# Weight sums on GpSimd instead of VectorE, with all units and loads in a new order: an attention and gated feed-forward kernel

## The chip, the cores and the metric

The kernel runs on one core of a Trainium2 chip. The metric is the device time of one execution in microseconds (us); three runs were made of the kernel before. A profile is one further execution, recorded instruction by instruction. PE is TensorE (matmuls), PEld its weight loads, DVE VectorE, ACT ScalarE, POOL GpSimd, SP SyncE, which here only issues DMAs.

## The reference

Eight batches with 12 heads of 448 tokens and 64 dimensions go through an attention without softmax, and the result through a gated feed-forward layer with exact GELU:

```
scores = (q @ k.T) / sqrt(64)
attn   = max(scores, 0) ** 2 / 448
x      = attn @ v                      # 12 heads x 64 = 768 columns, 3584 rows
out    = (gelu(x @ w_gate) * (x @ w_val)) @ w_out   # 768 -> 1536 -> 768
```

Inputs and output are float32; the kernel computes in bf16 with float32 accumulation.

## The kernel before, in words

**Attention.** For each batch `b`, heads are worked in pairs and in three groups `m` of four heads. q and k come by a casting DMA issued from GpSimd into `qk16`. They are transposed into `qkT`: for the first six groups by TensorE (line 683, against the identity `ident`) with a copy on VectorE or ScalarE (line 687), for the later ones by a regrouping copy on VectorE (line 511, `qkr`) and two DMA transposes issued by SP (line 516). A scores unit (`s` in the order, 21 per batch) makes 128 x 896 scores in PSUM; ScalarE applies relu (line 751), in batch 0 VectorE for the units in `RELU_V` (line 749); VectorE squares in place (line 770), two units in one instruction, in batch 0 only for the numbers in `PAIRED`. A values unit (`v`, one per head pair) multiplies by v; VectorE or ScalarE scales the result into `xT` (lines 829 and 841).

**Feed-forward.** All weights stay in SBUF: `w_gate` and `w_val` in six pieces `wg0..5`, `wv0..5` of 256 columns, loaded in pairs (`W` in the list of loads), and `w_out` in four pieces `wo0..3` (`O`). A digit in the order is a plain gate or value unit of that batch: gate ends in a GELU on ScalarE (line 1104), value in a product on VectorE into `uT` (line 1109). For batches 2 to 7 part of this work is done by a seven-product scheme on 2 x 2 blocks (units such as `2A1`): instead of eight block products seven are made, of sums of blocks. That needs sums of weights, `ws`: four per weight pair, made in `add_pair_sums` (line 905, 24 instructions of 128 x 768 in all), and sums of tokens, `ts` (line 934). The fourth sum of each pair is written over the upper half of `wv` itself, so it waits until the plain units that read that half are done.

**Output.** The product with `w_out` uses the same scheme in 14 groups `a` to `n` of 256 rows, seven units each; it needs sums of output weights, `wt` (line 1152, eight instructions of 128 x 1152, in two chains of four), and sums of `uT`, `s` (line 1236). ScalarE copies and VectorE adds into `osb` (lines 1319 and 1317), and SP stores it.

**TensorE.** Every matmul uses a 64 x 64 quarter of the array, four side by side; nearly all are recorded on line 401, in `mm`. Two streams, `PE0` and `PE1`, are interleaved: the lower half of one unit beside the upper half of another. Where nothing is ready in the first 24 us, `fill` issues matmuls on the zero tile `warm` (line 603) so that TensorE does not sit idle.

**What sets the order.** It is planned while the program is built. `START` and `LINE` list the units; `LOADS` lists the first DMAs, which GpSimd issues in order. `run_plan` simulates the engines with a cost per operation and emits each instruction on its engine when the plan says it starts; on the chip each engine then runs its instructions in that order, and semaphores hold it where an input is late. From 12 units ahead it takes the first that is ready. Loads of late batches are paced: each waits on GpSimd for a relu of an earlier batch (`op.behind`). A DMA transpose is taken to land 5 us after its issue (`lag=5.0`).

Of the kernel before, what the change touches and what calls it, by code (L numbers as in the profile page):

```python
# [12 lines left out]
s s s 0 0 s t s 0 s s v 0 s s s s t s v 0 0 0 v 0 s s s s s v s v 0 s s 0 s v 0 1 0 0 1 1 1 1 s 1 0  # L13
0 1 0 s s 1 0 s s s 1 s 1 1 w1 v s s 1 1 s 0 1 1 1 0 s 1 s s 0 1 0 s s 0 1 v 1 1 1 1 a1 s a2 s s s
a7 a6 1 v a4 s a5 v s b7 s b1 s b6 v w0 a3 s s b5 b4 b2 s v 2 s b3 s 2 s 2 s 2 v 2 s 2 s s s s v s
s s v 2 s 2 2 c1 c6 v c7 s s v 2 c2 c4 2 c5 s s 2 v s s 2A1 2D1 s 2A7 2D7 w2 2A2 2A6 c3 s s s 3 2D6
2A5 2A4 v 2D2 2D4 s 3 v 2D5 2F1 s 2E1 2F2 2A3 3 s 2F6 s 2D3 2E7 2F7 s 2E6 v 2E2 2E5 2E4 2E3 3 s 2C1
2F5 s 3 2C6 2F4 2B1 2C2 v 2C7 2B6 2B7 2C5 s s s 2F3 2B5 s 2C4 s 3 2C3 w3 s s s 2B2 s 2B4 3 2B3 3 d1
d7 d6 3 3 v v s s e1 s s e2 d5 e7 d4 d3 v d2 s s s e6 v s f7 3 s 3 s f1 e4 f6 s s f5 e5 s s 4 f4 4
v s s f3 v f2 4 4 v s s e3 s s 4 4 4 s s s g7 v 4A1 s g1 s s s s v v g6 4 5 s 4A7 4A2 4A6 g5 g2 g4  # L20
4D1 4A4 s s 4E1 4A5 4E2 v s 4A3 4D7 g3 4D6 4E6 s 4D5 4D2 5 4E7 4E4 s 4B1 4E5 s s 4F1 s 4B6 v 4D4
4D3 s s 4B7 v 4B2 4G1 4B5 4B4 s 4F6 4F7 4F2 4G6 4E3 4B3 4G2 s 4H1 s 4F5 4F4 4F3 4G7 v 4C1 s s 4H2
4H7 4G5 4H6 4G4 s 4H4 4H5 s 4G3 s 4C6 s v v 4C7 4C5 4C2 5 4C4 s s 4C3 s 5 5 h7 4H3 h1 s 5 5 s h6 s
h5 i1 5 i7 s i6 s v s s s h3 v i4 h2 6B1 h4 v 6A1 s s v 6B2 i5 i3 6A6 6A2 j1 j7 j2 i2 6A7 6B7 6D1
6G1 6A4 6B6 j6 j4 6A5 6B4 w4 6D7 j5 6D6 6B5 6G6 6G7 6A3 6D2 w5 6G5 j3 6G2 6C1 6C2 6B3 6C6 6D4 6E1
6D5 6E2 6C7 6H1 6G4 6C5 6C4 6E7 6D3 6G3 6E6 6H2 6L1 6H7 6E5 6H6 6H4 6K1 6H5 6C3 6L2 6K2 6L6 6E4 6K6
6L7 6L5 6H3 6K7 6F1 6I1 6E3 6F6 6F7 6J1 6F2 6K5 6K4 6F5 6L4 6I2 6I6 6F4 6J6 6I7 6L3 6J2 6J7 6K3 6F3
6I5 6I4 6J5 k7 6J4 6I3 6J3 l1 n1 l6 k1 k6 k5 k4 k3 l7 l4 m7 m1 m2 n7 n2 m6 l5 l3 n6 m4 m5 n5 n4 l2
m3 n3 k2
# [3 lines left out]
LOADS = "q8 v4 v8 W0 Q0 W1 Q1 V0 W2 V1 Q2 W3 V2 W4 W5 O0 O1 O2 O3"  # L33
# [3 lines left out]
t00a s0 s1 t01 s2 s3 s4 s5 s6 t10 s7 t11 s8 s9 s10 t20 t21 s11 v0 s12 s13 v1 s14 v2a s15 s16 x0 v3a  # L37
s17 x0 s18 x1 x1 x1 s19 v4a s20 f x0 x0 x0 x1 v5 t30
# [3 lines left out]
class Op:  # L42
# [4 lines left out]
    def __init__(self, engine, cost, emit, deps=(), lag=0.0, prio=0, other=None):  # L47
        self.serial = Op.count
        Op.count += 1
        self.engine, self.cost, self.emit, self.prio = engine, cost, emit, prio  # L50
        self.deps = [d for d in deps if d is not None]
        self.lag = lag
        self.other = other
        self.takes = None
        self.margin = 0.0
        self.after = None
        self.gate = 0.0
        self.hold = self.whole = False
        self.mark = None
        self.start = self.end = self.known = self.blocked = None  # L60
# [58 lines left out]
def run_plan(queues, pools, units, banks, full, arrivals, together, fill, blocks, span):  # L119

    free = {e: 0.0 for e in (*queues, *pools)}
    at = {e: 0 for e in queues}
# [4 lines left out]
    def ready(op):  # L129
        if op.known is not None:  # L130
            return op.known
        if op.blocked is not None and op.blocked.end is None:
            return None
        t = 0.0
        if op.after is not None:
            if op.after.start is None:
                return None
            t = op.after.start
        if op.takes is not None:
            x = op.takes[0].free(*op.takes[2:])  # L140
            if x is None:
                return None
            t = max(t, x)
        for d in op.deps:
            if d.end is None:
                op.blocked = d
                return None
            t = max(t, d.end + d.lag + (op.margin if d.engine == "SP" else 0.0))
        if op.gate:
            if not blocks.marks:  # L150
                return None
            at, _ = blocks.marks[-1]
            t = max(t, at, free[op.engine])
# [12 lines left out]
        return t  # L166
# [51 lines left out]
    while left:  # L218
# [16 lines left out]
        for e, ops in pools.items():  # L235
            mine = None
            for op in ops[:48]:
                r = ready(op)
                if r is not None:
                    t = max(r, free[e], floor if e in together else 0.0)  # L240
                    key = (t, op.prio, free[e])
# [38 lines left out]
        free[e] = op.end  # L280
# [27 lines left out]
def kernel(  # L308
# [38 lines left out]
    PAIRED = (0, 7)  # L347
    RELU_V = (0, 16)
    GATE_T, BLOCK = 0, 7.1

    NPB = (0,0,3,3,4,4,6,6)
    TWO = 2, 4, 6
# [5 lines left out]
    RING_M, RING_G = 5, 4  # L358

# [20 lines left out]
           for i in range(FB)]  # L380
    early = tc.tile_pool(name="psS1", bufs=1, space=bass.MemoryType.PSUM)
    psS.append(early.__enter__())

    ctx.enter_context(tc.manual_schedule())

    ident = const.tile([128, 128], bf16)
    warm = const.tile([128, 512], bf16, name="warm")
# [22 lines left out]
    ACT, DVE, POOL, SP, IDLE = [], [], [], [], []  # L410
# [91 lines left out]
    def add_dma_transposes(b, m, deps=()):  # L502
# [34 lines left out]
        if m and b == EARLY:  # L537
            tr_op[b, m][0].deps.append(tr_op[b, m - 1][1])
# [9 lines left out]
    held, readers, until, shut = {}, {}, {k: 0.01 * k - 1e3 for k in range(FB)}, {}  # L548
# [13 lines left out]
    def new_bank(k, reader, shape=(128, 512), dtype=f32):  # L562
        if k >= FB and len(psF) == FB:
# [6 lines left out]
    def next_scores(at):  # L570

        n = len(units)
        if n >= WIDE and n % SB == 0 or wide:
# [5 lines left out]
        return n % SB, units[n - SB:n - SB + 1]  # L579

    def scores_read(n, reader):
        units.append(reader)
        if n == 1:
            for k in (FB, FB + 1):
                readers[k] = [reader]

    def fill(t0, t1):
# [3 lines left out]
        at_rest = {k: -1.0 if held.get(k) is None else held[k].end for k in (*range(FB), *held)}  # L591
# [288 lines left out]
    def add_pair_sums(i):  # L880
# [18 lines left out]
        for n, x, y, op in ((1, lambda: a21, lambda: a22, ALU.add),  # L899
# [5 lines left out]
            have = [Op("DVE", 0.53, lambda n=n, x=x, y=y, op=op: nc.vector.tensor_tensor(  # L905
                made(n), x(), y(), op=op), have, lag=0.2, prio=3)]
            ws_op[n, i] = have[0]
            DVE.extend(have)
# [15 lines left out]
    def add_token_sums(b):  # L924
# [3 lines left out]
        def emit(n, x, y, op):  # L928
# [5 lines left out]
            nc.vector.tensor_tensor(ts[b, n][:, :, :], x, y, op=op)  # L934

        b11, b12, b21, b22 = (b0, KTOP, c0), (b1, KTOP, c1), (b0, KEND, c0), (b1, KEND, c1)
        for n, x, y, op, on in ((3, b22, b12, ALU.subtract, []), (1, b12, b11, ALU.subtract, [3]),
# [4 lines left out]
            made = Op("DVE", 0.83 if b in TWO else 0.48, lambda n=n, x=x, y=y, op=op: emit(n, x, y, op),  # L942
# [8 lines left out]
            DVE.append(made)  # L951
# [3 lines left out]
    def add_pair(at, b, unit, name):  # L955
# [8 lines left out]
        if name in opens:  # L964
            st["box", stage] = {}
            free = []
        else:
            free = [st["read", stage]]
# [13 lines left out]
        def emit(r, k):  # L982
# [62 lines left out]
        if name in "167":  # L1045
# [19 lines left out]
        then(at, GS, *ops, box if name in opens else None, lambda: st["read", stages_last[stage]])  # L1065
# [73 lines left out]
    def add_weight_sums():  # L1139

        for i in range(2):
# [6 lines left out]
            for n, out_, x, y, op in ((3, wt[3, i][:, :, :], b22, b12, ALU.subtract),  # L1148
# [3 lines left out]
                done = Op("DVE", 0.75, lambda out_=out_, x=x, y=y, op=op: nc.vector.tensor_tensor(  # L1152
# [3 lines left out]
                DVE.append(done)  # L1156
# [39 lines left out]
    def add_sums(gr):  # L1196
# [26 lines left out]
        def add(n, x, y, op, into=None, after=(), cuts=(0, KH)):  # L1223
# [3 lines left out]
            def emit(f0, f1):  # L1227
# [4 lines left out]
                for j in ((0, 1) if split else (None,)):  # L1232
# [3 lines left out]
                    nc.vector.tensor_tensor(st["tile"][n][:, f0:f1, cols], a, c, op=op)  # L1236

            for f0, f1 in zip(cuts, cuts[1:]):
# [161 lines left out]
    for n, (b, m) in enumerate(late):  # L1400
# [3 lines left out]
        for b_, m_ in late[n - 1:n] + (late[n:] if n == len(late) - 1 else []):  # L1404
            load_v(b_, 4 * m_, 4 * m_ + 4)
# [7 lines left out]
    flow_t = [(1, m, (0, 1)) for m in range(1, FIRST_T - NM)]  # L1413
# [154 lines left out]
    run_plan({"PE0": PE0, "POOL": POOL}, {"PE1": PE1, "ACT": ACT, "DVE": DVE, "SP": SP, "IDLE": IDLE}, later,  # L1568
# [34 lines left out]
```

## Time and profile before

| what | value |
|---|---|
| runs | 395.8, 395.2, 395.75 us; median 395.75 |
| profiled execution, span from first to last instruction | 397.0 us |
| PE busy | 388.1 us, 98% |
| DVE busy | 297.5 us, 75% |
| ACT busy | 268.5 us, 68% |
| POOL busy | 95.7 us, 24%, nearly all of it issue of DMAs |
| moved by DMA | 44.82 MB, mean 113 GB/s |

The profiled execution's own device time is not given apart from its span, which lies 1.25 us above the median of the runs. A busy PE is not a PE at full rate, since matmuls overlap; the number of matmuls in a stretch of time says more. The granted clock is 1.00 nearly throughout.

### The profile page before, as it was taken

The page shows a single profiled execution, that of the slowest core. Times are in us where ns is not written, and L with a number is a line of the kernel's source. Part 1 is how long each engine was busy: PE and PEld are TensorE (multiplying, and loading weights), DVE is VectorE, ACT ScalarE, POOL GpSimd, SP SyncE. Part 2 cuts the span into 40 slices and gives each one's busy share as a digit, 9 for nine tenths or more (in the row PEclk, how much of TensorE's full clock was granted, in tenths as well). Part 3 has the DMA queues.
Part 4 walks back from the last instruction along what each step waited for, and adds up shares of the span by engine and source line. Part 5 has one row for each costly group of instructions (what it writes and reads, how often), then busy time and mean ns, then how long its engine had stood idle before and what let it go on. Part 6 is the DMA issues. An engine that isn't in the chain of part 4 may idle for free.

```text
span 397.0 us, 18156 instructions
## 1 busy us (share of the span) xinstructions
PE 388.1 (98%) x8195; PEld 335.3 (84%) x8198; DVE 297.5 (75%) x479; ACT 268.5 (68%) x428; POOL 95.7 (24%) x156
## 2 busy tenths in 40 slices
PE   7999999999999999999999999999999999999995
PEld 3355689978988998899999989889999998899994
DVE  2695795767797688889878669698999577778652
ACT  2795872266687778988577787889877656665320
POOL 5755523322233333123123333130100000000000
PEclk9999999999999999999999999999999999999999
DMA  7999999998989999856588998964302240000055
GB/s 91 168 200 198 197 207 201 93 117 105 122 152 152 199 110 179 107 73 97 71 138 144 140 200 123 146 94 56 50 2 62 64 122 2 4 3 2 23 142 160
DMA packets 76333, 44.82 MB, mean 113 GB/s; under 512 B 36832, under 2 KB 73184, under 8 KB 76256
## 3 DMA queue, kind: packets, MB, share of 16 engines
q0 software_dynamic: 37728, 24.39, 47.7%
q1 hardware_dynamic: 37888, 18.49, 26.4%
q8 instruction: 64, 1.05, 1.1%
q10 hardware_dynamic: 640, 0.79, 0.7%
q14 instruction: 13, 0.11, 0.1%
HBM read 48.76 MB, written 11.01 MB: 151 GB/s over the span
## 4 chain that ended last, share of the span: by engine, by line
PE 81%; DMA 15%; POOL 1%; issue 1%; ACT 1%; DVE 0%; SPq 0%; ACTq 0%; POOLq 0%; DVEq 0%
PE ff L401 71%; PE sp L401 8%; DMA qk<-in_k_dram 5%; DMA wg<-in_moe_w_gate_dram 3%; DMA wv<-in_moe_w_val_dram 3%; DMA qkT<-qkr 2%; PE ff L603 1%; DMA v<-in_v_dram 1%; DMA out_dram<-osb 1%; PE ff L683 1%; POOL v L479 0%; POOL wg L440 0%; SPq L516 0%; PE ff L645 0%; ACT attnT L751 0%
## 5 line engine op out<-in xcount | busy, mean ns | idle before, releaser
L401 PE MATMUL ff<-xT,wg 64*64 64x448 bf16 x1680 | 179.8, 349 | 0.4 <-ACT xT L841 0.4
L751 ACT ACTIVATE attnT<-sp 128x896 bf16<-128x896 f32 x148 | 134.0, 921 | 31.0 <-PE sp L401 30.4
L401 PE MATMUL ff<-xT,wv 64*64 64x448 bf16 x1056 | 114.4, 349 | 0.0
L401 PEld LDWEIGHTS <-wg 64*64 64x64 bf16 x1680 | 101.2, 107 | 9.7 <-issue 0.9
L401 PEld LDWEIGHTS <-wv 64*64 64x64 bf16 x1680 | 101.5, 107 | 9.0
L770 DVE TENSOR_TENSOR attnT<-attnT 128x1792 bf16<-128x1792 bf16 (+1 forms) x84 | 82.1, 987 | 15.0 <-ACT attnT L751 14.8
L401 PEld LDWEIGHTS <-s 64*64 64x64 bf16 x1344 | 77.8, 107 | 4.6 <-issue 0.4
L401 PE MATMUL sp<-qkT 64*64 64x448 bf16 x672 | 78.3, 358 | 1.2 <-DMA qkT<-qkr 0.4
L401 PE MATMUL ff<-attnT,v 64*64 64x448 bf16 x600 | 74.0, 350 | 0.2 <-DVE attnT L770 0.2
L401 PE MATMUL ff<-xT,ws 64*64 64x448 bf16 x624 | 71.1, 349 | 0.0
L401 PE MATMUL ff<-ts,wv 64*64 64x448 bf16 x624 | 68.8, 349 | 0.0
L401 PE MATMUL ff<-wo,s 64*64 64x384 bf16 x672 | 62.4, 323 | 0.0
L401 PE MATMUL ff<-wt,s 64*64 64x384 bf16 x672 | 60.9, 323 | 0.0
L401 PEld LDWEIGHTS <-ws 64*64 64x64 bf16 x936 | 56.0, 107 | 3.9
L1011 DVE TENSOR_TENSOR part<-ff,part 128x448 f32<-128x448 f32 x78 | 47.4, 622 | 15.4 <-PE ff L401 11.1
L401 PEld LDWEIGHTS <-uT 64*64 64x64 bf16 x912 | 55.8, 107 | 2.7
L401 PE MATMUL ff<-wo,uT 64*64 64x384 bf16 x576 | 55.3, 322 | 0.0
L460 POOL DMA_DIRECT2D qk<-in_q_dram x43 | 26.6, 620 | 96.7 <-ACT attnT L751 76.4
L401 PEld LDWEIGHTS <-v 64*64 64x64 bf16 x672 | 40.7, 107 | 6.0 <-issue 1.3
L1007 ACT COPY part<-ff 128x448 f32<-128x448 f32 x78 | 40.2, 539 | 7.9 <-PE ff L401 6.1
L1319 ACT COPY osb<-ff 128x384 f32<-128x384 f32 x56 | 26.6, 482 | 28.0 <-PE ff L401 22.5
L1109 DVE TENSOR_TENSOR uT<-gel,ff 128x448 bf16<-128x448 bf16 x44 | 27.2, 620 | 20.7 <-PE ff L401 18.0
(69 smaller groups left out, 471.4 us busy)
## 6 DMA issues: line engine op xcount, KB each, us to landing
out_dram<-osb SPq DMA_DIRECT2D x48, 192.0 KB, 3.7
v<-in_v_dram POOLq DMA_DIRECT2D x48, 128.0 KB, 5.3
qk<-in_q_dram POOLq DMA_DIRECT2D x38, 112.0 KB, 3.9
qk<-in_k_dram POOLq DMA_DIRECT2D x38, 112.0 KB, 4.2
wg<-in_moe_w_gate_dram POOLq DMA_DIRECT2D x6, 384.0 KB, 9.5
wv<-in_moe_w_val_dram POOLq DMA_DIRECT2D x6, 384.0 KB, 10.9
wo<-in_moe_w_out_dram POOLq DMA_DIRECT2D x4, 576.0 KB, 14.7
qk<-in_q_dram POOLq DMA_DIRECT2D x5, 224.0 KB, 7.0
```

Of the source, the lines that this page charges most:

```text
L401: ins = nc.tensor.matmul(o, lhsT, rhs, start=start, stop=stop, skip_group_check=onto, tile_position=(P * row, P * col))
L460: return nc.gpsimd.dma_start(qk16[b, m][HALF[i], g0 - 4 * m:g1 - 4 * m, :], src[b, g0:g1].rearrange("h (p c) d -> p h (c d)", c=SC))
L603: blocks.add(nc.tensor.matmul(t[:, 0:cols], warm[:, 0:128], warm[:, 0:cols], start=True, stop=True))
L683: blocks.add(nc.tensor.transpose(t[HALF[j], c, :], src[:, 2 * r + j, c, :], ident[:, :], tile_position=(0, P * j)))
L751: relu.ins = nc.scalar.activation(o, x, AF.Relu).ins
L770: nc.vector.tensor_tensor(a[:, part], a[:, part], a[:, part], op=ALU.mult)
L1007: rd.ins = nc.scalar.copy(st["t", name][:, :], box[0][:, 0:S]).ins
L1011: rd.ins = nc.vector.tensor_tensor(t[:, :], box[0][:, 0:S], t[:, :], op=ALU.add).ins
L1109: u_op[b, fc].ins = nc.vector.tensor_tensor(uT[b][:, fc, :], gel.pop((b, fc))[:, :], box[0][:, 0:S], op=ALU.mult).ins
L1319: ins = nc.scalar.copy(o, box[0][:, 0:OGS])
```

## The change

Four things change. The numbers of matmuls and of sums stay as they were.

1. `ws` and `wt` sums, 24 and 8 instructions, are issued on GpSimd (`nc.gpsimd.tensor_tensor`) instead of VectorE. A new pool `GP` in the planner shares GpSimd's time with the list of loads: the loads stay in order among themselves, and the sums are placed between them when their inputs are there. The planner takes 1.8 and 2.6 us for them on GpSimd.
2. `START`, `LINE` and `LOADS` have a new order. In `START`, v3 is scaled on VectorE instead of ScalarE and v5 the other way round. Among the loads v of heads 8 to 11 of batch 0 goes behind `W0` and `Q0`, and the weight pairs come as 0, 2, 1, 3, 5, 4.
3. In batch 0 one more relu is on VectorE (unit 2), and two more pairs of squares are joined (numbers 1 and 8).
4. In the planner a DMA transpose now lands 5 us after its issue plus the backlog of loads, at most 9 us more, and adds to that backlog. `ident` and `warm` become parts of the first tile of the output ring instead of tiles of their own.

The settings `TRICK` and `SB3` are 0, so what they switch is not used; `ts` and `osum` sums stay on VectorE, since `ON_POOL` does not name them.

```diff
-LOADS = "q8 v4 v8 W0 Q0 W1 Q1 V0 W2 V1 Q2 W3 V2 W4 W5 O0 O1 O2 O3"
+LOADS = "q8 v4 W0 Q0 v8 Q1 W2 V0 W1 Q2 V1 W3 W5 V2 O0 W4 O2 O3 O1"

 START = """
-t00a s0 s1 t01 s2 s3 s4 s5 s6 t10 s7 t11 s8 s9 s10 t20 t21 s11 v0 s12 s13 v1 s14 v2a s15 s16 x0 v3a
-s17 x0 s18 x1 x1 x1 s19 v4a s20 f x0 x0 x0 x1 v5 t30
+t00a s0 s1 t01 s2 s3 s4 s5 s6 t10 s7 t11 s8 s9 s10 t21 s11 v0 t20 s12 s13 v1 s14 v2a s15 x0 s16 v3
+s17 s18 x1 s19 s20 v4a x1 x1 x0 x0 x0 f x0 x1 v5a t30
 """
...
-                t = max(r, free[e], floor if e in together else 0.0)
+                t = max(r, free[same[e]], floor if e in together else 0.0)
...
+        if op.crowd:
+            op.lag = 5.0 + min(9.0, max(0.0, dma - t - 1.5))
+            if dma > t + 1.5:
+                dma += 2.4
...
-    PAIRED = (0, 7)
-    RELU_V = (0, 16)
+    PAIRED = (0, 1, 7, 8)
+    RELU_V = (0, 2, 16)
...
+    ON_POOL = ("ws", "wt",)
+    POOL_COST = dict(ws=1.8, wt=2.6, ts=3.0, tsh=1.6, osum=(0.25, 0.29))
...
-    ident = const.tile([128, 128], bf16)
-    warm = const.tile([128, 512], bf16, name="warm")
+    first = opool.tile([TT, 2 * d_model], bf16, name="osb", tag="osb")
+    warm, ident = first[:, 0:512], first[:, 512:640]
...
+    def placed(kind, cost, pool_cost, *args, **kw):
+        on = kind in ON_POOL
+        op = Op("GP" if on else "DVE", pool_cost if on else cost, *args, **kw)
+        (GP if on else DVE).append(op)
+        return op
+
+    def elementwise(kind):
+        return nc.gpsimd if kind in ON_POOL else nc.vector
...
-            have = [Op("DVE", 0.53, lambda n=n, x=x, y=y, op=op: nc.vector.tensor_tensor(
+            have = [placed("ws", 0.53, POOL_COST["ws"], lambda n=n, x=x, y=y, op=op: elementwise("ws").tensor_tensor(
                 made(n), x(), y(), op=op), have, lag=0.2, prio=3)]
...
-                done = Op("DVE", 0.75, lambda out_=out_, x=x, y=y, op=op: nc.vector.tensor_tensor(
+                done = placed("wt", 0.75, POOL_COST["wt"], lambda out_=out_, x=x, y=y, op=op: elementwise("wt").tensor_tensor(
                     out_, x, y, op=op), have, lag=0.2, prio=2)
...
-    run_plan({"PE0": PE0, "POOL": POOL}, {"PE1": PE1, "ACT": ACT, "DVE": DVE, "SP": SP, "IDLE": IDLE}, later,
+    run_plan({"PE0": PE0, "POOL": POOL}, {"PE1": PE1, "ACT": ACT, "DVE": DVE, "SP": SP, "IDLE": IDLE, "GP": GP}, later,
```

The 17 lines of `LINE` are replaced by 17 others with the same units; the first of each:

```diff
-s s s 0 0 s t s 0 s s v 0 s s s s t s v 0 0 0 v 0 s s s s s v s v 0 s s 0 s v 0 1 0 0 1 1 1 1 s 1 0
+s s s 0 0 0 0 s v t 0 s s s s s s t s 0 0 0 s v 0 s 0 s s v 0 0 s 0 s v s 0 s v 0 s s s 0 v s s s s
```

More of the change, by code (lines that the diff above doesn't have):

```diff
@@ L18 @@
[L18 to L28, printed above, removed]
@@ L57, in __init__ @@
         self.gate = 0.0
-        self.hold = self.whole = False
+        self.hold = self.whole = self.crowd = False
         self.mark = None
@@ L119, in run_plan @@
 def run_plan(queues, pools, units, banks, full, arrivals, together, fill, blocks, span):
+    same = {e: "POOL" if e == "GP" else e for e in (*queues, *pools)}
     free = {e: 0.0 for e in (*queues, *pools)}
@@ L562, in new_bank @@
     def new_bank(k, reader, shape=(128, 512), dtype=f32):
+        if psF[min(k, FB - 1)] is None:
+            third.__exit__(None, None, None)
+            psF[2:] = [ctx.enter_context(
+                tc.tile_pool(name=f"psF{i}", bufs=1, space=bass.MemoryType.PSUM, side="right"))
+                for i in (2, 3)]
         if k >= FB and len(psF) == FB:
@@ L572, in next_scores @@
         n = len(units)
-        if n >= WIDE and n % SB == 0 or wide:
+        n0 = NU if SB3 else 0
+        if SB3 and n < NU + 2:
+            return n % 3 if n < NU else n - NU, units[max(n - 3, 0):n - 2] if n >= 3 else []
+        if n >= WIDE and (n - n0) % SB == 0 or wide:
             if not wide:
@@ L578, in next_scores @@
             return 0, units[-1:]
-        return n % SB, units[n - SB:n - SB + 1]
+        return (n - n0) % SB, units[n - SB:n - SB + 1]
     def scores_read(n, reader):
         units.append(reader)
+        if SB3 and len(units) == NU:
+            for k in (2, 3):
+                readers[k] = [reader]
+                until[k] = 0.01 * k - 1e3
         if n == 1:
@@ L590, in fill @@
             return
-        at_rest = {k: -1.0 if held.get(k) is None else held[k].end for k in (*range(FB), *held)}
+        at_rest = {k: -1.0 if held.get(k) is None else held[k].end for k in (*range(FB), *held)
+                   if k >= FB or psF[k] is not None}
         at_rest = {k: end for k, end in at_rest.items() if end is not None}
@@ L963, in add_pair @@
         stage = stages[name]
-        if name in opens:
+        onto = TRICK and name == "2"
+        opening = name in opens and not onto
+        if opening:
             st["box", stage] = {}
@@ L967, in add_pair @@
         else:
-            free = [st["read", stage]]
+            free = [st["read", "1" if onto else stage]]
+        if TRICK and name == "1":
+            st["box", "Z"] = {}
         box = st["box", stage]
@@ L989, in emit @@
             o = blocks[f] * 128 % WCH
+            if TRICK and name == "1" and r == 0 and k == 0:
+                z = st["box", "Z"]
+                z[0] = new_bank(z["k"], st["read", "1"])
+                if "cover" in z:
+                    for j in range(2):
+                        mm(z[0][HALF[j], OGS:S], a()[HALF[0], c, o + P * j:o + P * (j + 1)], mov[HALF[0], c, 0:S - OGS],
+                           0, j, False, True, True)
             for j in range(2):
@@ L999, in add_pair @@
         last = ops[1][-1]
+        if TRICK and name == "1":
+            ops[0][0].deps += [x_op[b0, dc] for dc in range(KC)[KEND]]
         if isinstance(x, int):
@@ L1043, in mult @@
             return m
-        if name in "167":
+        if TRICK and name == "1":
+            rd = Op("ACT", 0.5, emit_onto, [last], lag=0.2, prio=0)
+            ACT.append(rd)
+        elif onto:
+            rd = gelu(lambda: box[0][:, 0:S], [last], 0.06)
+        elif name in "167":
             rd = Op("ACT", 0.5, emit_copy, [last], lag=0.2, prio=0)
@@ L1064, in add_pair @@
             mult("3", "7", b1, c1, st["sum", "5"], st["half"])
-        then(at, GS, *ops, box if name in opens else None, lambda: st["read", stages_last[stage]])
+        then(at, GS, *ops, box if opening else None, lambda: st["read", stages_last[stage]],
+             (st["box", "Z"], lambda: st["read", "2"]) if TRICK and name == "1" else None)
     opened = {}
```

67 lines of the change are left out of this document (42 added, 25 removed).

## The prediction

> **What bounds the kernel now.** I read the page's first lines and its chain of waits, then TensorE's work by stretches, then the places where that work falls short.
>
> ```profile
> span 397.0 us, 18156 instructions
> PE 388.1 (98%) x8195; PEld 335.3 (84%) x8198; DVE 297.5 (75%) x479; ACT 268.5 (68%) x428; POOL 95.7 (24%) x156
> PE 81%; DMA 15%; POOL 1%; issue 1%; ACT 1%; DVE 0%; SPq 0%; ACTq 0%; POOLq 0%; DVEq 0%
> ```
>
> The chain that ended last is 81% TensorE and 0% VectorE: the engine that gets relief is not the one that sets the end. Since overlapped matmuls make "busy" say little, I count the matmuls of line 401 (all but transposes and warm-up) in stretches of 10 us; the columns are stretch, length, busy time with count, granted clock, DMA share, GB/s.
>
> ```profile
> 20.00:30.00 10.00, 9.10 (x132) 1.00 1.38 200
> 30.00:40.00 10.00, 7.89 (x139) 1.00 1.40 198
> 50.00:60.00 10.00, 10.00 (x219) 1.00 1.25 208
> 80.00:90.00 10.00, 9.56 (x201) 1.00 1.16 115
> 110.00:120.00 10.00, 10.00 (x224) 1.00 1.01 175
> 120.00:130.00 10.00, 10.00 (x213) 1.00 1.30 140
> ```
>
> A full stretch of 448-column matmuls holds 219, or 45.7 ns each. Against that, 20 to 30 us lacks 87 (4.0 us), 30 to 40 us lacks 80 (3.7 us, some of it transposes), and 80 to 90 us lacks 18 (0.8 us). So the start loses most, and later there are only small holes. The counts of 110 to 130 us hold narrower matmuls of 384 columns, those with `wo` and `wt`:
>
> ```profile
> 110.00:120.00 10.00, 6.83 (x91) 1.00 1.01 175
> 110.00:120.00 10.00, 5.38 (x60) 1.00 1.01 175
> 120.00:130.00 10.00, 2.86 (x29) 1.00 1.30 140
> ```
>
> At 384/448 of 45.7 ns, 39.2 ns, the first stretch is 151 narrow and 73 wide, 9.3 us of work; the second 29 and 184, 9.5 us. They lose 0.7 and 0.5 us. All that a new order can win back after the start is thus 0.8 + 1.2 = 2.0 us.
>
> **The sums that move.** Their cost on VectorE:
>
> ```profile
> L905 DVE TENSOR_TENSOR ws<-wg,ws 128x768 bf16<-128x768 bf16 x6 | 3.3, 554 | 0.1
> L1152 DVE TENSOR_TENSOR wt<-wo,wt 128x1152 bf16<-128x1152 bf16 x2 | 1.5, 754 | 0.0
> masks.py:199 POOL TENSOR_SCALAR_AFFINE_SELECT ident<-ident 128x128 bf16<-128x128 bf16 x1 | 0.3, 287 | 0.1
> ```
>
> VectorE loses 4 x 3.3 for the gate and value sums and 4 x 1.5 for the output sums (of each kind three more groups like the one shown): 19.2 us of 297.5. By itself that is worth nothing to the end, for the chain holds next to no VectorE; it is worth something only where VectorE is late, which the next two parts cost. On GpSimd no sum of two tensors was profiled. The nearest row takes 287 ns for 128 elements: 2.24 ns each, so 768 cost 1.72 us and 1152 cost 2.58 us, if nothing of the 287 is a fixed price. The lower end is VectorE's 0.55 and 0.75. I take the upper end, since that row is the only computation of GpSimd: 24 x 1.72 + 8 x 2.58 = 61.9 us. Put on POOL's 95.7 us that is 158 of 397, so GpSimd does not become the bound; a chain of four output sums grows from 3.0 to 10.3 us.
>
> **The hole at 82 us** (−0.8 us). The transposes as a group (median us to landing), one row of VectorE's order in time, and the chain of waits between 60 and 90 us:
>
> ```profile
> qkT<-qkr SPq DMA_TRANSPOSE x36, 4.5
> 68.85 0.75 DVE L1152 TENSOR_TENSOR wo<-wo 128x1152 bf16<-128x1152 bf16 x1
> 71.19 0.75 DVE wt L1152
> 71.94 0.55 DVE qkr L511
> ...
> 73.94 9.23 DMA qkT<-qkr
> ...
> 83.22 0.57 PE sp L401 x8
> ```
>
> The scores of batch 2 wait for two transposes by DMA, of which the second, issued by SP at 73.9, landed 9.2 us later (the median of 36 is 4.5 us), while q, k and v loads cross them. Ahead of the copy that starts them stands an output sum on VectorE. From 68.85 to 71.94 us VectorE ran three such sums, 2.25 us. With them gone the copy can go up to 2.2 us sooner, enough to cover the 0.8 us; and the planner now takes a transpose as 5 us plus the backlog of loads instead of 5, which puts gate and value units ahead of these scores. Either alone closes the hole. Bounds: −0.8 to 0, as the loads are reordered too. I take −0.8.
>
> **The holes of 110 to 130 us** (−0.4 us). Here VectorE is crowded:
>
> ```profile
> 110.00:115.00 5.00, 5.00 (x127) 4.57 (x123) 4.84 (x9) 5.00 (x8) 3.23 (x5) 1.00 0.70 133
> 118.22 0.55 DVE L905 TENSOR_TENSOR ws<-wv 128x768 bf16<-128x768 bf16 x1
> ...
> 125.62 0.55 DVE L905 TENSOR_TENSOR wv<-wg,wv 128x768 bf16<-128x768 bf16 x1
> ```
>
> The third and fourth numbers after the length are PEld and DVE: VectorE is at 4.84 of 5 us and ScalarE at 5.00. Four weight sums, 2.2 us, follow in the crowd. Bounds: −1.2 (both holes go) to 0 (ScalarE is as full, and another order meets the same crowd elsewhere). I take a third.
>
> **The start** (−0.5 us).
>
> ```profile
> 20.00:30.00 10.00, 9.35 (x135) 5.03 (x135) 9.45 (x16) 8.93 (x13) 5.33 (x8) 1.00 1.38 200
> 11.01 2.48 POOL L479 DMA_DIRECT2D v<-in_v_dram  x4
> 13.41 0.91 POOL L440 DMA_DIRECT2D wg<-in_moe_w_gate_dram  x1
> 24.16 0.35 PE L401 MATMUL ff<-xT,wg 64*64 64x448 bf16 x2
> L749 DVE TENSOR_SCALAR attnT<-sp 128x896 bf16<-128x896 f32 x2 | 2.2, 1088 | 1.1 <-PE sp L401 1.1
> L770 DVE TENSOR_TENSOR attnT<-attnT 128x1792 bf16<-128x1792 bf16 x66 | 71.4, 1087 | 12.6 <-ACT attnT L751 12.3
> L770 DVE TENSOR_TENSOR attnT<-attnT 128x896 bf16<-128x896 bf16 x18 | 10.9, 622 | 2.4 <-ACT attnT L751 2.4
> L751 ACT ACTIVATE attnT<-sp 128x896 bf16<-128x896 f32 x148 | 134.0, 921 | 31.0 <-PE sp L401 30.4
> v<-in_v_dram POOLq DMA_DIRECT2D x48, 128.0 KB, 5.3
> qk<-in_q_dram POOLq DMA_DIRECT2D x5, 224.0 KB, 7.0
> ```
>
> From 20 to 30 us VectorE (9.45 of 10) and ScalarE (8.93) pass relu and square while DMA moves 200 GB/s. The first weights wait behind four v issues; two of them now come later, so 256 KB less stands ahead: 256/200 = 1.3 us sooner. The second pair of weights instead gets q and k of batch 1 ahead, 448 KB or 2.2 us later. One relu more goes to VectorE (1.09 there, 0.92 off ScalarE), two more pairs of squares are joined (2 x 0.62 becomes 1.09, 0.16 saved each, but the first half waits up to 0.92 for the second relu), and one copy changes place each way. VectorE gets 1.09 − 0.32 = 0.8 us more, ScalarE 0.9 less. Bounds: −2.5 us (1.3 and 0.9 both reach the end, with a little from the filler) to +2.2 (the late second weights all show). I take −0.5, nearer the middle, for the gate units begin at 24.16 us, where relu and square keep both engines full whenever the weights land.
>
> **GpSimd's queue, and VectorE beside it** (+0.3 us). Loads for later batches are issued by GpSimd in order and now stand behind sums. They wait long anyway:
>
> ```profile
> POOL qk L460 <- ACT attnT L751: 108.5, 49, 8.2
> POOL v L479 <- ACT attnT L751: 34.9, 23, 11.7
> ```
>
> GpSimd sits 143 us in 72 waits that only pace loads, 2 us each; one sum of 1.72 us fits inside most of them. The exception is a sum that itself waits (the last of four overwrites a value half and needs the units that still read it): loads behind it wait with it, up to the planner's error. Bounds 0 to 1.5 us (a late batch twice costs a hole like that at 82 us); with the rival below unseen in this trace I take 0.3 for both. `ident` and `warm` in one tile of the output ring cost nothing: the first output copy comes long after their last reader, the transposes.
>
> **The sum.** −0.8 − 0.4 − 0.5 + 0.3 = −1.4 us: a span of 395.6. The profiled execution stands 1.25 us over the runs' median of 395.75, so I forecast 394.35, rounded **394.3 us**. All bounds at once give −4.5 to +3.7, 391.2 to 399.4; as terms of separate stretches seldom all fall to one side, the forecast's own range is 392.5 to 396.
>
> **Rivals.** *GpSimd and VectorE hold each other up* (slower). While a sum reads its two tensors, VectorE instructions with two inputs in SBUF stand still. The squares take 71.4 + 10.9 us and the products into `uT` 31.3, together 114 of 397 us or 29%, so 62 us of GpSimd sums could hold VectorE for 18 us, about the 19.2 taken off, and for more where such instructions are dense. It decides where VectorE has no spare time: six groups of four sums, of which some fall in stretches like 110 to 115 us or
>
> ```profile
> 300.00:305.00 5.00, 5.00 (x125) 4.89 (x121) 5.00 (x9) 4.05 (x7) 0.00 (x0) 1.00 0.07 16
> L1020 DVE TENSOR_TENSOR uT<-gel,part 128x448 bf16<-128x448 bf16 x52 | 31.3, 620 | 3.7 <-ACT gel L1015 3.0
> ```
>
> If each group costs the 0.7 us that TensorE lost at 110 to 120 us, that is 4.2 us: 394.0 (the sum without the 0.3) + 4.2 = 398.2. Against it: at 300 to 305 us VectorE is full and TensorE lost nothing. The Trainium skill's page "SBUF — State Buffer", section "Who interferes with whom", states this lock: a VectorE instruction with two SBUF inputs and a GpSimd instruction that reads SBUF share a read port, and the second fully blocks. No GpSimd sum stands in this trace to test it; by that rule this rival holds, without it only the +0.3 is too much.
>
> *The start gains in full*: −2.5 instead of −0.5, 392.3. For it speaks that nearly 8 us are lost from 20 to 40 us; against it that relu and square, not loads, fill 20 to 30 us.
>
> *Nothing moves*: TensorE is the bound, the hole at 82 us opens somewhere else as the same bytes and transposes must pass, 395.7.
>
> *Loads late behind sums*: two batches cost 0.8 us each and the second weights 0.8: 394.3 + 2.4 = 396.7. Against it the 143 us of waits.
>
> *The sums cost twice as much on GpSimd* (124 us): it still fits under the span, and changes the time only through the first and fourth rival.
>
> **How the numbers follow.** Forecast 0.43, full start 0.17, nothing 0.14, mutual blocking 0.18, late loads 0.08. A measurement here tells 0.2%, 0.8 us, from no change. The forecast gives 0.37 to faster and, with its own weak end, 0.06 to same; the full start is faster; "nothing" gives 0.11 to same and 0.03 to slower, late loads 0.02 and 0.06, blocking 0.18 to slower: faster 0.54, same 0.19, slower 0.27. The range is cut at 391.4 and 398.2: below lies a start better than its bound, above a blocking worse than 0.7 us per group, one in ten each.
>
> **What would show it.** The hole at 82 us gone: 219 matmuls or nearly so from 80 to 90 us. VectorE near 278 us busy; joined squares still 1087 ns, the products into `uT` still 620. If these grow beside GpSimd's, or GpSimd's sums take well over 1.72 and 2.58 us, the blocking is real; if TensorE then lacks matmuls in those stretches, I am wrong. 20 to 40 us should hold some 10 matmuls more than 132 + 139 = 271; fewer than 260 would mean that the second weights came too late.

## The result, and the profile after

The changed kernel takes 424.08 us (median of four runs, 424.03 to 424.58) against 395.48 us (395.04 to 395.8) of the kernel before, timed beside it: a ratio of 1.0731, with an interval of 1.0717 to 1.0745. It is 28.6 us slower, where 394.3 us had been forecast and 398.2 us was the upper end.

The page of the profile after: span, busy time of each engine, the granted clock in 40 slices of 10.55 us, and the shares of the chain of waits.

```profile
span 422.0 us, 18162 instructions
PE 392.6 (93%) x8197; PEld 334.6 (79%) x8197; DVE 315.4 (75%) x447; ACT 267.1 (63%) x426; POOL 156.7 (37%) x188
PEclk9999999569999999999999999999988999999998
PE 72%; DMA 14%; DVE 7%; issue 5%; ACT 1%; POOL 0%; ACTq 0%; DVEq 0%; POOLq 0%
```

VectorE was relieved of 32 instructions (479 to 447) and yet is busy for 315.4 us instead of 297.5; it should have been near 278. It now holds 7% of the chain instead of nothing. The clock line dips in two places. TensorE's matmuls by stretches (line 412 is what line 401 was; stretch, length, busy with count, granted clock, DMA share, GB/s):

```profile
70.00:80.00 10.00, 1.30 (x26) 0.69 0.01 2
80.00:90.00 10.00, 2.75 (x32) 0.50 0.29 26
300.00:310.00 10.00, 7.50 (x126) 0.83 0.19 24
310.00:320.00 10.00, 7.19 (x124) 0.83 0.01 2
```

A full stretch holds 219 wide matmuls (or 255 narrow ones). From 70 to 90 us there are 58 in 20 us, and DMA moves 2 GB/s in the first half of it; from 300 to 320 us there are 250. Elsewhere TensorE is nearly full. **Two holes make the loss.** Counting every stretch as in the prediction (its length less its matmuls and transposes at their undisturbed price), I get what TensorE loses. The price here is about 47 ns for a wide matmul (28 in a row take 1.32 us in the chain of waits of before) and 40 for a narrow one, since the 219 behind the prediction's 45.7 ns include those that the edges of the stretch cut. In the table, the row "before, again" is a second profile of the kernel before, told of below.

| lost by TensorE, us | 0–40 | 40–70 | 70–90 | 90–140 | 140–300 | 300–340 | span |
|---|---|---|---|---|---|---|---|
| before | 20.5 | 0.5 | 1.1 | 2.0 | 2.7 | 0.7 | 397.0 |
| before, again | 17.5 | 0.5 | 1.6 | 2.0 | 2.7 | 0.7 | 394.6 |
| after | 17.3 | 0.5 | 17.7 | 3.1 | 3.4 | 10.0 | 422.0 |

Against the second profile, 16.1 us come at 70 to 90 and 9.3 at 300 to 340: 25.4 of the 27.4 us between the spans.

**The hole at 70 to 90 us.** VectorE's and then GpSimd's instructions in order of time (start, duration), and the row of the waits that names the hole:

```profile
67.79 18.88 DVE L531 COPY qkr<-qk 128x1792 bf16<-128x1792 bf16 x1
86.59 0.61 DVE L1163 TENSOR_TENSOR uT<-gel,ff 128x448 bf16<-128x448 bf16 x1
```

```profile
66.81 1.26 POOL L499 DMA_DIRECT2D v<-in_v_dram  x2
68.07 1.66 POOL L939 TENSOR_TENSOR ws<-ws,wg 128x768 bf16<-128x768 bf16 x1
69.67 1.65 POOL L939 TENSOR_TENSOR ws<-wv 128x768 bf16<-128x768 bf16 x1
...
83.84 2.35 POOL L1206 TENSOR_TENSOR wt<-wo,wo 128x1152 bf16<-128x1152 bf16 x1
87.20 1.25 POOL L480 DMA_DIRECT2D qk<-in_q_dram  x2 [1.02 <-issue]
```

```profile
PE ff L412 <- DVE uT L1163: 16.0, 1, 16.0
```

A copy that takes 0.6 us takes 18.88. It begins while GpSimd issues two loads; then ten sums follow with no gap (of 128 x 768 or 128 x 1152 elements), from 68.07 to 86.18, and the copy ends with them. The product into `uT` stands behind it on VectorE, and TensorE waits 16.0 us for that product. The next loads of q and k need the copy and stand behind the sums: they are issued at 87.20.

**The hole at 300 to 320 us.** VectorE, then GpSimd:

```profile
301.02 6.01 DVE L1068 TENSOR_TENSOR uT<-gel,part 128x448 bf16<-128x448 bf16 x3
306.96 2.52 DVE L804 TENSOR_TENSOR attnT<-attnT 128x1792 bf16<-128x1792 bf16 x1
309.41 0.61 DVE L1163 TENSOR_TENSOR uT<-gel,ff 128x448 bf16<-128x448 bf16 x1
309.94 3.37 DVE L1289 TENSOR_TENSOR s<-uT 128x768 bf16<-128x768 bf16 x2
```

```profile
300.34 4.24 POOL L939 TENSOR_TENSOR ws<-wv 128x768 bf16<-128x768 bf16 x2
304.54 4.00 POOL L939 TENSOR_TENSOR ws<-ws,wg 128x768 bf16<-128x768 bf16 x2
```

Here the two engines take turns, one instruction each. Three products take 2.0 us each instead of 0.62, a square 2.52 instead of 1.09, and a sum 2.0 instead of 1.65: each waits for the other's instruction to end. Only the product into `uT` of line 1163 is as quick as ever.

### The profile page after: what moved, and what is told of

The parts are those of the page before. It is cut to its first block, busy times and chain, and to the rows that moved or that the text cites. A ratio compares the mean times of both kernels' runs of the same rounds, so it can differ in the third digit from the quotient of the medians.

```text
span 422.0 us, 18162 instructions
## 1 busy us (share of the span) xinstructions
PE 392.6 (93%) x8197; PEld 334.6 (79%) x8197; DVE 315.4 (75%) x447; ACT 267.1 (63%) x426; POOL 156.7 (37%) x188
## 4 chain that ended last, share of the span: by engine, by line
PE 72%; DMA 14%; DVE 7%; issue 5%; ACT 1%; POOL 0%; ACTq 0%; DVEq 0%; POOLq 0%
PE ff L412 65%; PE sp L412 6%; DMA wv<-in_moe_w_val_dram 5%; DMA wo<-in_moe_w_out_dram 4%; DVE attnT L804 2%; DMA v<-in_v_dram 2%; DMA qk<-in_k_dram 2%; DVE uT L1068 2%; DVE s L1289 1%; DMA out_dram<-osb 1%; DVE uT L1163 1%; DVE attnT L783 1%; PE ff L637 0%; POOL qk L480 0%; DVE part L1059 0%
## 5 line engine op out<-in xcount | busy, mean ns | idle before, releaser
L412 PE MATMUL ff<-xT,wg 64*64 64x448 bf16 x1680 | 182.2, 353 | 16.0 <-DVE uT L1163 16.0
L412 PEld LDWEIGHTS <-wg 64*64 64x64 bf16 x1680 | 100.0, 108 | 28.4 <-issue 16.6
L412 PE MATMUL ff<-xT,wv 64*64 64x448 bf16 x1056 | 115.6, 352 | 0.0
L804 DVE TENSOR_TENSOR attnT<-attnT 128x1792 bf16<-128x1792 bf16 (+1 forms) x82 | 87.6, 1079 | 8.9 <-ACT attnT L785 8.9
L412 PE MATMUL sp<-qkT 64*64 64x448 bf16 x672 | 76.0, 353 | 1.2 <-ACT attnT L785 0.3
L412 PE MATMUL ff<-attnT,v 64*64 64x448 bf16 x600 | 76.2, 353 | 0.8 <-DVE attnT L804 0.7
L412 PE MATMUL ff<-ts,wv 64*64 64x448 bf16 x624 | 72.1, 349 | 0.0
L412 PE MATMUL ff<-wo,uT 64*64 64x384 bf16 x576 | 56.2, 337 | 2.3 <-DVE uT L1068 2.3
L1158 ACT ACTIVATE gel<-ff 128x448 bf16<-128x448 f32 x44 | 24.0, 546 | 38.7 <-PE ff L412 38.3
```

The source lines that it names most:

```text
L412: ins = nc.tensor.matmul(o, lhsT, rhs, start=start, stop=stop, skip_group_check=onto, tile_position=(P * row, P * col))
L804: nc.vector.tensor_tensor(a[:, part], a[:, part], a[:, part], op=ALU.mult)
L1158: nc.scalar.activation(gel[b, fc][:, :], box[0][:, 0:S], AF.Gelu)
```

## The experiments

All are built on the changed kernel. My theory after the traces was that the sums' engine makes both holes, by holding VectorE and by standing ahead of loads; its first rival was that the new order makes them.

**1. The new lists and planner, with all sums back on VectorE in the plan too.**

```diff
-    ON_POOL = ("ws", "wt",)
+    ON_POOL = ()
```

> The changed kernel with ON_POOL empty: new order, loads, relus and planner, but all 32 weight sums on VectorE again (the planner places them there). Theory A (the sums on GpSimd hold VectorE's instructions up; the copy of 18.88 us and the stretch of 300 to 315 us are that): both holes go, about 17.3 + 9.5 us less than 424.1, and what is left is the new order alone: 393 to 397 us. Theory B (the new order leaves TensorE without ready work, whoever forms the sums): still above 410 us. Theory C (the clock that fell after the first hole is a large part): no own forecast here, the granted clock would return to 1.00 with A.

Measured: 405.41 us (404.65 to 406.3), ratio 1.0238 (1.0208 to 1.0268). From 70 to 90 us TensorE loses 2.2 us, from 300 to 340 us 2.1: the holes are gone, but the time stays above the 393 to 397 us of theory A. A new assignment gives a new plan, whose smaller losses lie elsewhere (6.8 us from 140 to 300), so this run doesn't price the order of the changed kernel; run 5 does.

**2. The sums on GpSimd, with the old lists and settings.** `START` and `LINE` are the old ones too.

```diff
-LOADS = "q8 v4 W0 Q0 v8 Q1 W2 V0 W1 Q2 V1 W3 W5 V2 O0 W4 O2 O3 O1"
+LOADS = "q8 v4 v8 W0 Q0 W1 Q1 V0 W2 V1 Q2 W3 V2 W4 W5 O0 O1 O2 O3"
...
-    PAIRED = (0, 1, 7, 8)
-    RELU_V = (0, 2, 16)
+    PAIRED = (0, 7)
+    RELU_V = (0, 16)
...
-            op.crowd = True
+            op.crowd = False
```

> The sums on GpSimd with the order, loads, START, PAIRED and RELU_V of the kernel before, and transposes planned at 5 us as before. Theory A: it has sums behind one another on GpSimd where the first qkr copy of batch 2 is due (72 us before), so it too loses a large part: 405 to 425 us, with one copy of over 5 us. Theory B: about 396 us, as the order is the old one.

Measured: 428.67 us, slower than the 405 to 425 of theory A and as slow without the new order as with it. The holes lie at 70 to 80, 90 to 110 and 300 to 330 us. The copy of more than 5 us is there:

```profile
68.73 8.83 DVE L532 COPY qkr<-qk 128x1792 bf16<-128x1792 bf16 x1
```

It is held through five sums that run into each other and gets in at 77.07 us, where the next sum needs the result of the one before it and begins 0.08 us after that one's end; runs 6 and 10 add such waits elsewhere. VectorE at another place, two squares of 1.09 us each, and GpSimd beside them:

```profile
97.23 8.29 DVE L805 TENSOR_TENSOR attnT<-attnT 128x1792 bf16<-128x1792 bf16 x2
```

```profile
98.95 1.23 POOL L481 DMA_DIRECT2D qk<-in_q_dram  x2
100.15 1.22 POOL L481 DMA_DIRECT2D qk<-in_k_dram  x2
...
101.95 2.42 POOL L1207 TENSOR_TENSOR wt<-wo,wt 128x1152 bf16<-128x1152 bf16 x1
```

The second square, 5.65 of the 8.29 us, is held through a train of issues and through the sum behind it.

**3. The copies of batch 2 as an instruction with two inputs** (the larger of x and x, on VectorE), since the copy starved (it got in only behind the whole row) and instructions with two inputs took turns.

```diff
-            nc.vector.tensor_copy(
...
+            if b == EARLY:
+                nc.vector.tensor_tensor(o, x, x, op=ALU.max)
```

> The changed kernel, but the three regrouping copies of batch 2 are VectorE tensor_tensor maximum of the tile with itself, in the same place of VectorE's order. Theory A in the form that only the plain copy starves behind a row of sums, while an instruction with two inputs gets in between two sums (squares took about one sum longer, 2.2 instead of 1.09 us): the first copy takes 1.6 to 4 us, the hole at 70 to 87 us falls from 17 to at most 3 us, and the time is 407 to 412 us. If any VectorE instruction that needs the shared access starves behind that row: 424 us as before, with a tensor_tensor of some 18 us. Theory B: 424 us.

Measured: 425.29 us, and in VectorE's order of time:

```profile
68.54 19.41 DVE L534 TENSOR_TENSOR qkr<-qk 128x1792 bf16<-128x1792 bf16 x1
```

It starves just as long. The kind of instruction isn't what tells the two places apart.

**4. The copies of batch 2 on ScalarE.**

```diff
+            if b == EARLY:
+                nc.scalar.copy(o, x)
```

> The changed kernel, but the three regrouping copies of batch 2 are on ScalarE, planned in the same place. Theory A: ScalarE is held up by nobody; the copy takes about 2 us, the hole at 70 to 87 us goes, 406 to 410 us, while the hole at 300 to 315 us stays with about 9 us. Theory B: 424 us.

Measured: 425.0 us, where theory A had 406 to 410. TensorE's stretches:

```profile
70.00:80.00 10.00, 10.00 (x220) 1.00 0.65 83
80.00:90.00 10.00, 2.21 (x46) 0.75 0.32 49
90.00:100.00 10.00, 5.18 (x72) 0.56 0.54 74
```

TensorE runs full to 80 us, and then has the hole all the same. The chain of waits names what it is:

```profile
68.45 9.63 POOL ws L942 x6
78.08 2.32 POOL wt L1209
...
87.19 1.16 POOL qk L480 x2
...
92.27 1.69 ACT qkr L534
```

The copies are done by 72.8 us, so the next q and k could be loaded, but GpSimd issues them only at 86.6, behind the row of sums. The held copy, for which TensorE waited 16.0 us in the changed kernel, and the late loads lie over each other: with the first taken away, the second costs as much. The held copy with the loads on time can't be had, since the loads need the copy. Three products with one input in PSUM (line 1166) ran beside this row, at 69.65, 71.92 and 77.59 us, and took 0.62 us each as ever.

**5. The plan of the changed kernel, instruction for instruction, with the sums issued by VectorE.** Unlike run 1 this leaves TensorE's order as it is.

```diff
     def elementwise(kind):
-        return nc.gpsimd if kind in ON_POOL else nc.vector
+        return nc.vector
```

> The plan and TensorE's order are those of the changed kernel; only the 32 sums are issued by VectorE instead of GpSimd. Theory A (the sums' engine alone makes the two holes): the copy into qkr at about 68 us takes 0.7 us or less, the loads of the next batch are issued near 71 us, and from the span after of 422.0 the losses of 70 to 90 us (17.4), of 300 to 320 us (9.5) and about 1 us of drag go: span 394 to 395, time 396 to 397. Theory B (the new order of units and loads makes them): the holes stay at their places, time above 410.

Measured: 399.14 us (396.6 to 401.02), ratio 1.0085 (1.0059 to 1.0111); the profiled execution took 397.51 us with a span of 395.7. That is 2 us more than expected, and the ten runs scatter over 4.4 us, which nothing here explains.

```profile
68.56 0.62 DVE L531 COPY qkr<-qk 128x1792 bf16<-128x1792 bf16 x1
```

```profile
69.71 1.19 POOL L480 DMA_DIRECT2D qk<-in_q_dram  x2 [2.44 <-DVE qkr L531]
```

Copy and loads are where the theory put them; the losses are 0.9 us from 70 to 90 and 0.5 from 300 to 340. So some 25 of the 28.6 us are the engine of the sums and nothing else. What is left, 0.85%, belongs to the rest of the change (order, loads, relus, planner), which this run doesn't take apart.

**6. Each sum waits for the end of the sum before it.**

```diff
+            def emit_waiting():
+                ins = emit_sum()
+                if sum_before:
+                    tc.add_manual_dep(ins.ins, sum_before[0].ins.name, SYNC, reason="pace")
+                sum_before[:] = [ins]
```

> Each sum on GpSimd waits for the end of the sum before it; the plan is that of the changed kernel. Theory A1 (VectorE is let in whenever a sum truly starts afresh, and in the row at 68 us it is not, since the sums run into each other): the copy at 68 us takes at most 2.3 us, one sum and itself. Theory A2 (VectorE is held as long as any sum is queued behind, whatever they wait for): the copy takes 17 us or more again. In both the next batch's loads still stand behind the row of sums in GpSimd's order, so the time stays 420 to 426 us.

Measured: 423.66 us. VectorE:

```profile
68.23 2.52 DVE L543 COPY qkr<-qk 128x1792 bf16<-128x1792 bf16 x1
...
71.21 1.53 DVE L543 COPY qkr<-qk 128x1792 bf16<-128x1792 bf16 x1
```

The copies get in after one sum, 2.52 us (2.3 had been the bound of theory A1) and 1.53 instead of 18.9. As expected the time doesn't gain by it: the hole moves to 80 to 110 us, since the loads still stand behind the sums, as in run 4.

**7. The first sums go behind the six loads of a batch** (`v_loads[2, 2]`).

```diff
+            args = [lambda: emit_sum() if open_gate else waiting.append(emit_sum), *args]
...
+            if op in v_loads.get((2, 2), ())[-1:]:
+                open_gate.append(1)
+                for emit_sum in waiting:
+                    emit_sum()
```

> The sums of the first group are issued on GpSimd only behind the six loads of the batch after next; all else as in the changed kernel. Theory A (copy held by the sums, and loads behind the sums, are the two causes of the hole at 70 to 90 us, and either alone keeps it): with both taken away the 17.4 us go except a little: 406 to 408 us; the hole at 300 to 320 us stays at 9 to 10 us. Theory B (one of the two suffices and is not taken away here, or the sums are now late for the units that need them): the hole moves and the time stays above 415.

Measured: 431.62 us, a miss for the 406 to 408. From 70 to 90 us TensorE loses 0.2 us, so with copy and loads ahead of the sums that hole is gone. But the six loads are those issued from 81.55 to 86.86 us, one group later than I had meant, and the chain runs on through the sums:

```profile
86.88 1.71 POOL ws L948
88.66 10.62 POOL ws L948 x6
99.29 3.17 POOL wt L1215
...
104.90 10.12 POOL wt L1215 x4
...
115.06 0.54 PE ff L412 x4
```

TensorE uses its first `wt` at 102.7 us, in run 5 at 97.8, and then sits idle twice for later ones, 8.7 us in all, the second time until 115 us. From 90 to 140 us 26.4 us are lost. The second branch of theory B holds, though that isn't the whole loss: squares and sums `s` on VectorE take turns with this row as well. It also shows how tight the plan is here: from 65 us on it places eight `ws` and eight `wt` sums, 8 x 1.65 + 8 x 2.36 = 32 us, and most of them ahead of the first use of `wt`, with twelve issues of loads between 69 and 87 us (run 5). The `ws` among them aren't used before 149 us there.

**8. The eight sums of weight pairs 4 and 5 on VectorE.**

```diff
-lambda n=n, x=x, y=y, op=op: elementwise("ws").tensor_tensor(
+lambda n=n, x=x, y=y, op=op: (nc.vector if i >= ROOM else nc.gpsimd).tensor_tensor(
```

> The eight sums of the weight pairs 4 and 5 (those at 300 to 315 us) are issued by VectorE, all others by GpSimd, plan unchanged. Theory A (one sum for one VectorE instruction, in turn, makes the hole at 300 to 320 us): that hole goes, products at 301 us take 0.62 instead of 2.06 us, the time falls by 8 to 9.5 us to 414 to 416. Theory B (the hole is there because VectorE has too much to do by plan at that place): it stays, time above 420.

Measured: 415.71 us, 8.4 us less than after. From 300 to 320 us TensorE holds 468 matmuls instead of 250, the loss of 300 to 340 us falls from 10.0 to 0.8, and the products there take what they took before, in VectorE's order of time:

```profile
302.49 0.62 DVE L1068 TENSOR_TENSOR uT<-gel,part 128x448 bf16<-128x448 bf16 x1
303.02 0.55 DVE L939 TENSOR_TENSOR ws<-wv 128x768 bf16<-128x768 bf16 x1
```

VectorE does the sum itself in 0.55 us and has time for it. What it hasn't is time to stand still for GpSimd's 1.65.

**9. The kernel before, unchanged, for a second profile.**

> The kernel before, unchanged, for a second profile. Theory A (the profiled execution of before, with a span of 397.0 us, was a slow one whose start ran at a low granted clock until 14 us): the first 40 us lose 17 to 17.6 us of TensorE's work instead of 20.5, the span is 393.5 to 394.8 us. Theory B (the first 40 us of before are slower than those of the changed kernel by its order): 20 us or more are lost again.

Measured: 396.38 us with a span of 394.6 us; in 40 us it loses 17.5 us, as the changed kernel does (17.3). TensorE's order of time in the start, first in the profile of the prediction, then in this one:

```profile
5.68 0.96 PE L645 MATMUL ff<-ident,qk 128*64 128x128 bf16 x14 [0.87 <-DMA qk<-in_k_dram]
...
8.55 0.96 PE L683 MATMUL ff<-ident,qk 128*64 128x128 bf16 x14
```

```profile
5.14 0.96 PE L645 MATMUL ff<-ident,qk 128*64 128x128 bf16 x14 [0.32 <-DMA qk<-in_k_dram]
...
7.73 0.58 PE L683 MATMUL ff<-ident,qk 128*64 128x128 bf16 x14
```

The losses and the span are those of theory A. Its reason isn't shown: the granted clock reads 1.00 up to 14 us in both profiles. In the first, k came 0.5 us later, TensorE sat idle for 0.87 us instead of 0.32, and the second transposes still took 0.96 us. That execution lost 3 us in its start that no other profile here shows, the one with the old `START` (run 2, 17.2 us) included.

**10. In each row only the second sum waits for the one before it.**

```diff
+                if len(row) == 1:
+                    tc.add_manual_dep(ins.ins, row[0].ins.name, SYNC, reason="pace")
+                row.append(ins)
...
             ins = emit()
+            row.clear()
```

> In each row of sums on GpSimd only the second waits for the end of the one before it; the others follow as in the changed kernel. Theory A1 (the row that starts behind transfers' issues is out of step, and one true wait brings it into step): the first copy at 68 us takes 2.5 us as where all sums wait, and the second, near 71 us, 1.5 to 2.3. Theory A2 (VectorE is let in only at a sum that waits): the first copy takes 2.5 us, the second is held for most of the row, 12 us or more. Loads still behind the sums: time 420 to 426 us in both.

Measured: 426.93 us, 1 us above the range. GpSimd, then VectorE:

```profile
68.62 1.66 POOL L952 TENSOR_TENSOR ws<-ws,wg 128x768 bf16<-128x768 bf16 x1
70.35 1.91 POOL L952 TENSOR_TENSOR ws<-wv 128x768 bf16<-128x768 bf16 x1
72.22 2.02 POOL L952 TENSOR_TENSOR ws<-wg,ws 128x768 bf16<-128x768 bf16 x1
```

```profile
68.01 2.76 DVE L544 COPY qkr<-qk 128x1792 bf16<-128x1792 bf16 x1
...
71.22 1.53 DVE L544 COPY qkr<-qk 128x1792 bf16<-128x1792 bf16 x1
```

The sum at 70.35 waits, and the first copy gets in ahead of it. The sum at 72.22 doesn't wait (it begins 0.04 us before the one before it ends; in the changed kernel's row each does so by 0.03 to 0.06 us), and the second copy gets in all the same, in 1.53 us. One true wait at the head of the row is enough to bring it from starving to taking turns: theory A1. The copy in run 2, let in at the first wait of its row, agrees.

**11. All three places mended:** `ws` of pairs 0 to 3 on GpSimd behind the loads of run 7, `wt` and pairs 4 and 5 on VectorE. Beside the edits of runs 7 (for `ws` alone) and 8:

```diff
-        return nc.gpsimd if kind in ON_POOL else nc.vector
+        return nc.gpsimd if kind == "ws" else nc.vector
```

> Of the 32 sums, the 16 of the weight pairs 0 to 3 into ws stay on GpSimd, behind the six loads of one batch; the eight into wt and the eight of the pairs 4 and 5 are issued by VectorE; the plan is that of the changed kernel. Theory A (the hole at 70 to 90 us comes from the copy and the loads that the sums hold, that of the run with the loads first from wt being late for units due at 98 us, that of 300 to 320 us from sums and VectorE in turn, and nothing else counts): all three go, 397 to 401 us, the level of the same plan on VectorE. Theory B (sums on GpSimd cost time wherever they stand): above 405.

Measured: 407.93 us (407.24 to 408.85), ratio 1.0318 (1.029 to 1.0346). It misses theory A by 7 us. The losses of 70 to 90 (0.9) and 300 to 340 us (0.5) are gone, but 11.9 us are lost from 90 to 140 instead of the 3.2 of run 5. TensorE waits for no sum now, but the row stands beside a new stretch of VectorE:

```profile
96.88 2.05 DVE L540 COPY qkr<-qk 128x1792 bf16<-128x1792 bf16 x1
98.86 2.52 DVE L813 TENSOR_TENSOR attnT<-attnT 128x1792 bf16<-128x1792 bf16 x1
```

Twelve sums from 87 to 114 us take turns with copies, squares and sums `s`. They also stand ahead of the next six loads and among them, so that these are issued from 106.85 to 114.9 us instead of 94.2 to 102.0 (run 5). The chain of waits from 84 to 130 us names instructions of VectorE and no transfer, so the turns are the likely cause, but no run separates the two. Theory B is nearer: this row costs in its new place too.

**12. Only the lone sums on GpSimd:** pair 3, and the last sum of pairs 0 to 2.

```diff
-        return nc.gpsimd if kind in ON_POOL else nc.vector
+        return nc.vector
...
-lambda n=n, x=x, y=y, op=op: elementwise("ws").tensor_tensor(
+lambda n=n, x=x, y=y, op=op: (nc.gpsimd if i == 3 or n == 3 and i < 3 else nc.vector).tensor_tensor(
```

> Of the 32 sums, seven stay on GpSimd: the four of weight pair 3 and the last of pairs 0, 1 and 2, which stand alone or two in a row between 108 and 190 us in the changed kernel; the other 25 are issued by VectorE; the plan is that of the changed kernel. Theory A (only rows of sums cost time; a lone one holds at most one VectorE instruction for 0.1 to 1.6 us and TensorE loses next to nothing): 397 to 401 us, the level of the same plan wholly on VectorE, 1.0085 of before. Theory B (each sum on GpSimd costs TensorE about as much as it holds VectorE): 402 to 406 us.

Measured: 397.22 us (396.74 to 397.65), ratio 1.0044 (1.0027 to 1.0061): theory A. Single VectorE instructions are held for up to 1.45 us beside a sum, and TensorE loses hardly more (8.6 us from 40 to 340 us, run 5 8.2). That this run is faster than run 5 lies within the scatter of the latter. It is still not below the kernel before, and no run points to a version that is.

## Why the prediction was wrong

**The price and load of the sums: right.** Undisturbed they take 1.62 to 1.66 and 2.35 us where 1.72 and 2.58 were forecast, and GpSimd is busy for 156.7 us (158). The one row of 287 ns served well.

**"GpSimd's queue, and VectorE beside it (+0.3 us)": the step that failed.** It measures about +25 us (run 5 against after). Both halves were mis-sized, and the rivals that held them were as well. For the queue I set 143 us of pacing waits, 2 us each, against single sums. But a mean over 397 us says nothing about the place where the plan puts the sums: eleven of them, 20 us, from 65 to 86 us, on an engine that must issue two groups of loads between 69 and 87 us. In the prediction I used the three output sums that VectorE runs at 68.85 to 71.94 us in the trace of before, and didn't ask what they become on GpSimd just there. *Loads late behind sums* was given 0.8 us per batch; run 4 puts it at the size of the whole hole.

*GpSimd and VectorE hold each other up* was the right mechanism, at 0.7 us per group of four. The groups don't cost alike. Lone sums cost nothing (run 12), the eight at 300 us cost 8.4 us (run 8), the first row, with the loads behind it, 16. VectorE loses 315.4 − 278 = 37 us where I had worked out 18 from a share of 29%. Half of it is one line, before and after:

```profile
L511 DVE COPY qkr<-qk 128x1792 bf16<-128x1792 bf16 x18 | 11.3, 626 | 0.8 <-DMA qkT<-qkr 0.7
L531 DVE COPY qkr<-qk 128x1792 bf16<-128x1792 bf16 x18 | 29.5, 1640 | 0.0
```

These copies have one input in SBUF and stood in none of my 114 us, which held two-input instructions alone; so I had no term for the one that cost most. The other 19 us are near the 18, in part by luck: the share took an instruction as held for the part of a sum that overlaps it, but where they take turns, each held instruction pays the rest of a sum, 1.4 us, whatever its own length. The signs that I had named for blocking are there: joined squares grow from 1087 to 1174 ns on average, products from 620 to 728. And "VectorE is full and TensorE lost nothing" at 300 to 305 us was put against the rival when it spoke for it: a full VectorE has no time in which it can be held.

**The hole at 82 us (−0.8)** closes by the new order, but elsewhere another opens: with the sums of the same plan on VectorE (run 5) 80 to 90 us loses 0.3 instead of 1.0 us, 100 to 110 us 1.4 instead of 0.4. **The holes at 110 to 130 us (−0.4)** lose 1.4 us in the second profile of before, 1.4 in run 5, 1.3 after. Both gains fall out, as the rival *nothing moves* had it.

**The start (−0.5)** gains 0.2 us, 17.5 against 17.3, which one profile each doesn't tell from nothing. The sign that I had named misleads: 20 to 40 us hold 306 matmuls instead of 271, but 302 in the second profile of before. The 7.7 us at 20 to 40 us that I weighed were partly of one execution: its start ran late by 3 us. For the same reason the sentence on 1.25 us was misread: device time lies about 1.9 us above the span (396.38 against 394.6, 424.03 against 422.0), so that execution stood some 3 us above the median. This hardly changes the forecast, which is in effect the median of the runs less the 1.4 us of the sum.

**The order itself** (with what else changed beside it) costs 0.4 to 0.9% (runs 12 and 5) instead of gaining 0.4. The runs don't settle which of its parts does.

## What to carry to other kernels

Before work is moved to GpSimd, count it in the window where it falls due, together with the DMA issues that the same engine owes in that window, not over the whole span. Lone instructions with two SBUF inputs cost next to nothing there; a row of them can make each VectorE copy, or instruction with two inputs in SBUF, wait for the rest of one of GpSimd's or even for the entire row, so a full VectorE gets fuller by giving work away. And take a second profile before a term of the sum rests on the first microseconds of one.

## What the runs showed of the hardware

A VectorE instruction can be held not by one instruction of GpSimd but by ten in a row: 18.88 us in the changed kernel, 19.41 with two inputs (run 3). This happened where the row followed DMA issues without a wait; a true wait ended it (run 2, after five sums) or brought it to turns of one for one from the start (run 10), and at 300 us, where the first sum itself had to wait for a square, it took turns from the start. What inside GpSimd makes the difference is open. The Trainium skill's page "SBUF — State Buffer", section "Who interferes with whom", says that the port is held for one whole instruction and the other side blocks fully; the turns at 300 us agree (2.0 us for 0.62), the row at 68 us goes beyond it.

Products with one input in PSUM (`uT<-gel,ff`) were not held: 0.61 us at 309.41, beside a sum, and 0.62 beside the row of run 4. By the same section a VectorE instruction with at most one SBUF input doesn't contend as long as it is outside the two-port performance modes, which agrees. The copies have one SBUF input too and were held; in which mode they ran no run shows.

In the first hole the granted clock falls too, to 0.69 from 70 to 80 and 0.50 from 80 to 90 us; the 32 matmuls after the restart at 87.25 us took 2.75 us, the time of nearly 60 at 47 ns, which puts about 1.3 us on top of the wait.
